# Loading parameter rows after the first transposes of x, and moving tile 7's first slabs, in a gated SSM + MLP kernel

## The chip, the cores and the metric

The kernel runs on one core of a Trainium2 chip. The metric is the device time of one execution in microseconds (us). A trace's span is 1.3 to 1.4 us shorter than the time of the same execution.

## The reference, cut to what matters

```
x: 2048 x 640, bf16                       # D = P = 640, F = 1728
g = sigmoid((x * gate_w).sum(-1))
dt = exp(log_dt); Lam_bar = exp(dt * (Lambda_re + i Lambda_im))
h[t] = Lam_bar * h[t-1] + (B_bar @ x[t])           # diagonal complex scan
a = 2 * Re(C @ h) + Dskip * x
b = gelu_tanh(x @ w1 + b1) @ w2 + b2
return g * a + (1 - g) * b
```

The parameters `Lambda_re`, `Lambda_im`, `log_dt` and `b1` are vectors. The kernel needs them as columns (one value per partition), so it loads them as rows and lets TensorE transpose them. A slab below is 128 of the 640 columns of x, or the 128 rows of w1 that go with them; a bank is one of the pieces of PSUM, the memory into which TensorE writes its results; a tile is one 128 x 512 result of the first product, kept in one bank.

## The kernel before: the parts that the change touches

Work is emitted by a list scheduler. Each `op(name, engine, modelled duration, reads, writes, emitter, prio)` becomes available when its inputs are, by modelled times; each engine takes the available op with the lowest `prio`. The order on each engine is therefore decided when the program is built, not on the chip.

The SyncE queue issues the large transfers in this order: x slabs 0 and 1 in natural layout, slabs 0 to 2 of W1 (256 KB each), then x slabs 2 to 4 by one DMA that transposes, then the rest of W1. ScalarE's queue issues the parameter rows at the very start.

```
load("xna", "sp", ...)                       # x[0:512], slabs 0 and 1, natural layout
w1load(0, "sp", 1); w1load(1, "sp", 1.3); w1load(2, "sp", 2)
xtrans(0, range(KN, KD), 3, 1.8)             # KN = 2: slabs 2..4 by a transposing DMA
w1load(3, "sp", 4); w1load(4, "sp", 5)
...
ROWS = {"lre": (0, A_Lambda_re), "lim": (KP, A_Lambda_im), "ldt": (2 * KP, A_log_dt), "b1a": (3 * KP, B_b1[0:nmain])}
op("rz", "pool", 0.2, (), list(ROWS) + ["b1b"], f_rz, prio=-90)            # zero the row tile
for i, (nm, (r0, src)) in enumerate(ROWS.items()):
    src = src.rearrange("(k p) -> k p", p=128)
    load(nm, "act", "l_" + nm, rows[r0:r0 + src.shape[0], :], src, [nm], prio=-100 + i, dur=0.4)
load("b1b", "pool", "l_b1b", rows[RT:RT + 1, :]..., ["b1b"], prio=-50, dur=1.0)   # tail of b1, as one more row
...
for i, (k, c0, c1) in enumerate(((0, 0, 2), (0, 2, 4), (1, 0, 4))):
    ...   # TensorE transposes x slabs 0 and 1 (8 blocks) into banks 7, 6, 5; VectorE copies them to xT
...
psC = PS[7][:, :].bitcast(BF16)[:, 0:128]
op("cols", "pe", 0.3, list(ROWS) + ["b1b", "ident"], [("bank", 7)], f_cols, prio=11.5)     # parameter transpose
op("cols1", "dve", 0.2, [("bank", 7)], ["lcol", "b1col"], f_cols1, prio=-1000)             # copy out of bank 7
op("dt", "act", ...)    # exp        then "ang" (VectorE), "amag" (exp), "psi" (VectorE), "sin" (two sines)
...
def m1_first():          # tiles 0..7 of x[0:512] @ W1, slab by slab, one PSUM bank per tile
    seq = [(k, jf) for k in range(KD) for jf in range(NW)]       # 5 slabs x 8 tiles = 40 matmuls
    seq.remove((0, NW - 1))
    seq.insert(seq.index((1, NW - 1)), (0, NW - 1))
    ...
    # then one GELU per tile on ScalarE; each frees its bank
```

The parameter transpose writes bank 7, which tile 7 also accumulates in, so tile 7 must wait until VectorE has copied the columns out. The ninth tile ("tile 8") reuses bank 0, so it must wait until the first GELU has read tile 0. And the exponentials and sines stand ahead of the first GELU on ScalarE, with two loads of the function table between them.

## Time and profile before

| | before |
|---|---|
| time, median of the runs (range) | 213.74 us (213.12 to 213.87) |
| TensorE busy | 209.3 of 212.3 us |
| parameter transpose starts | 7.61 us |
| first GELU starts | 12.62 us |
| tile 8 starts | 13.92 us |

The first line of the page's busy table (us, share of the span, instructions; PE is TensorE's matmuls, PEld its weight loads, DVE VectorE, ACT ScalarE, POOL GpSimd):

```profile
PE 209.3 (99%) x1264; PEld 120.6 (57%) x1264; DVE 189.2 (89%) x262; ACT 111.3 (52%) x201; POOL 3.0 (1%) x11
```

The waits of TensorE in the kernel before (engine, line, releaser: us in total, times, longest):

```profile
PE ps L399 <- PEq L960: 0.8, 1, 0.8
```

TensorE is the bound and waits for nothing once it has started. Its timeline over the first 15 us (start us, us, engine, line, operation, out<-in, shape, count):

```profile
3.75 1.03 PE L411 MATMUL ps<-ident,xn 128*128 128x128 bf16 x8
4.74 3.03 PE L619 MATMUL ps<-xT,W1sb 128*128 128x512 bf16 x11
7.61 0.22 PE L430 MATMUL ps<-ident,rows 128*128 128x128 bf16 x1
7.67 6.42 PE L619 MATMUL ps<-xT,W1sb 128*128 128x512 bf16 x29
13.92 1.24 PE L639 MATMUL ps<-xT,W1sb 128*128 128x512 bf16 x5
```

Eight transposes of x, 11 matmuls of the first pass, the parameter transpose, the other 29 matmuls, then tile 8 at 13.92.

The same stretch on ScalarE (a bracket gives the idle time before a line and its releaser; ACTq is ScalarE issuing a DMA):

```profile
0.97 0.55 ACTq L326 DMA_DIRECT2D rows<-in_A_Lambda_re_dram  x1
2.20 0.35 ACTq L326 DMA_DIRECT2D rows<-in_B_b_dram  x1
...
8.09 0.21 ACT L440 ACTIVATE dtb<-cols 128x5 bf16<-128x5 f32 x1 [4.23 <-DVE cols L435]
...
8.83 1.28 ACT L473 ACT_TABLE_LOAD   x1
...
10.78 1.28 ACT L628 ACT_TABLE_LOAD   x1
12.62 3.00 ACT L628 ACTIVATE Gl<-ps,cols 128x512 bf16<-128x512 f32 x5 [0.56 <-PE ps L619]
```

ScalarE was ready for the GELUs 0.56 us before TensorE had the first tile ready. The GELU ended at 13.30, 0.62 us before tile 8 needed its bank.

### The profile page before, as it was taken

What the parts mean: (1) busy time and instruction counts of PE and PEld (TensorE: products, weight loads), DVE (VectorE), ACT (ScalarE), POOL (GpSimd) and SP (SyncE); (2) the same over time, 40 slices, a digit from 0 to 9 for tenths busy, and PEclk for the clock granted to TensorE, in tenths of its full rate; (3) what the DMA queues carried; (4) which work ended last, traced back from release to release, by engine and by line L of the source; (5) the groups of instructions that cost most, each with busy time, mean ns of one, the idle gap of its engine ahead of it and who ended that gap; (6) DMA issues with size and microseconds to landing.
All of it is one profiled execution on the core that took longest, in us unless ns stands there. A gap on an engine that the chain in (4) does not pass through costs nothing.

```text
span 212.3 us, 3122 instructions
## 1 busy us (share of the span) xinstructions
PE 209.3 (99%) x1264; PEld 120.6 (57%) x1264; DVE 189.2 (89%) x262; ACT 111.3 (52%) x201; POOL 3.0 (1%) x11
## 2 busy tenths in 40 slices
PE   8999999999999999999999999999999999999995
PEld 3444444444567776444466777444446777767773
DVE  2499999999999999999999969899999999899443
ACT  2489556678905234556953233556792444722330
POOL 2000000000000010000000001000000000000000
DMA  5999799997000004100000014000000000010011
GB/s 147 316 263 203 161 221 317 274 213 173 24 0 3 31 31 127 62 0 0 0 3 0 0 36 154 31 31 3 0 0 2 3 31 31 31 34 0 31 34 62
DMA packets 31318, 16.35 MB, mean 77 GB/s; under 512 B 22984, under 2 KB 30408, under 8 KB 31304
## 3 DMA queue, kind: packets, MB, share of 16 engines
q1 hardware_dynamic: 30928, 14.83, 27.4%
q0 software_dynamic: 320, 1.31, 2.0%
q8 instruction: 10, 0.16, 0.3%
q14 instruction: 4, 0.03, 0.1%
q10 hardware_dynamic: 56, 0.01, 0.0%
HBM read 7.63 MB, written 2.62 MB: 48 GB/s over the span
## 4 chain that ended last, share of the span: by engine, by line
PE 99%; DVE 0%; issue 0%
PE ps L769 27%; PE ps L639 22%; PE ps L817 20%; PE ps L682 20%; PE ps L619 4%; PE ps L399 1%; PE ps L783 1%; PE ps L660 1%; PE ps L411 0%; DVE osb L850 0%; PE ps L430 0%
## 5 line engine op out<-in xcount | busy, mean ns | idle before, releaser
L769 PE MATMUL ps<-W2sb,Gl 128*128 128x320 bf16 x416 | 59.2, 299 | 0.0
L769 PEld LDWEIGHTS ps<-W2sb,Gl 128*128 128x128 bf16 x416 | 40.4, 98 | 17.0 <-issue 1.1
L639 PE MATMUL ps<-xT,W1sb 128*128 128x512 bf16 x220 | 48.1, 379 | 0.0
L817 PE MATMUL ps<-CT,H 128*128 128x320 bf16 (+2 forms) x320 | 45.4, 299 | 0.0
L722 DVE TENSOR_TENSOR_SCAN W<-atab,V 128x1280 bf16<-128x1280 f32 x16 | 44.3, 2811 | 0.3
L682 PE MATMUL ps<-xT,BT 128*128 128x512 bf16 x200 | 43.8, 379 | 0.0
L817 PEld LDWEIGHTS ps<-CT,H 128*128 128x128 bf16 x320 | 31.3, 98 | 12.2
L797 ACT ACTIVATE E<-ps,g1col 128x320 bf16<-128x320 f32 x32 | 16.3, 527 | 39.7 <-PE ps L769 25.5
L639 PEld LDWEIGHTS ps<-xT,W1sb 128*128 128x128 bf16 x220 | 21.6, 98 | 25.9
L646 ACT ACTIVATE Gl<-ps,cols 128x512 bf16<-128x512 f32 x44 | 29.6, 689 | 10.0 <-PE ps L639 10.0
L682 PEld LDWEIGHTS ps<-xT,BT 128*128 128x128 bf16 x200 | 19.4, 98 | 23.5 <-ACT Gt L668 0.4
L691 ACT ACTIVATE U<-ps 128x512 bf16<-128x512 f32 x40 | 23.8, 597 | 14.9 <-PE ps L682 14.9
L828 ACT ACTIVATE E<-ps,gcol 128x320 bf16<-128x320 f32 x30 | 15.8, 527 | 22.6 <-PE ps L817 22.6
L756 ACT ACTIVATE ps<-b2b 128x320 f32<-128x320 bf16 x32 | 14.1, 442 | 1.1
L480 DVE TENSOR_TENSOR osb<-xg,E 128x640 bf16<-128x640 bf16 x15 | 7.3, 488 | 7.9 <-ACT E L828 7.5
L836 DVE SCALAR_TENSOR_TENSOR xg<-xn,gcol,dsk 128x640 bf16<-128x640 bf16 x16 | 13.9, 883 | 0.4
L596 DVE SCALAR_TENSOR_TENSOR scr<-xn,gwb 128x640 bf16<-128x640 bf16 x16 | 13.2, 823 | 0.4
L480 DVE TENSOR_TENSOR V<-V,W 128x1280 bf16<-128x1280 bf16 x16 | 12.5, 821 | 0.3
L480 DVE TENSOR_TENSOR H<-H,V 128x1280 bf16<-128x1280 bf16 x16 | 12.5, 821 | 0.3
L480 DVE TENSOR_TENSOR V<-mr,U 128x2560 bf16<-128x2560 bf16 x8 | 11.9, 1489 | 0.2
L480 DVE TENSOR_TENSOR H<-c,W 128x2560 bf16<-128x2560 bf16 x8 | 11.9, 1490 | 0.2
L480 DVE TENSOR_TENSOR V<-s,W 128x2560 bf16<-128x2560 bf16 x8 | 11.9, 1484 | 0.0
(80 smaller groups left out, 100.2 us busy)
## 6 DMA issues: line engine op xcount, KB each, us to landing
out_dram<-osb SPq DMA_DIRECT2D x15, 160.0 KB, 1.8
W2sb<-in_B_w_dram SPq DMA_DIRECT2D x1, 2080.0 KB, 9.2
W1sb<-in_B_w_dram SPq DMA_DIRECT2D x5, 256.0 KB, 4.8
xn<-in_A_x_dram POOLq DMA_DIRECT2D x2, 640.0 KB, 4.7
xn<-in_A_x_dram SPq DMA_DIRECT2D x1, 640.0 KB, 7.7
W1sb<-in_B_w_dram SPq DMA_DIRECT2D x1, 480.0 KB, 5.8
W1sb<-in_B_w_dram SPq DMA_DIRECT2D x1, 400.0 KB, 6.4
xn<-in_A_x_dram SPq DMA_DIRECT2D x1, 384.0 KB, 6.0
```

Source lines behind the costliest of these rows:

```text
L480: return inc("dve", nc.vector.tensor_tensor(out=o, in0=a, in1=b, op=o_))
L639: t = nc.tensor.matmul(PS[bank][:, :], W1sb[:, k, jf * 128:(jf + 1) * 128], xT[q][:, k, :], start=(k == 0), stop=(k == KD - 1))
L646: return inc("act", nc.scalar.activation(Gl[q % 2][:, jf, :], PS[bank][:, :], ACT.Gelu_apprx_tanh, bias=b1col[:, jf:jf + 1]))
L682: t = nc.tensor.matmul(PS[bank][:, :], BT[:, ci, kd, k * 128:(k + 1) * 128], xT[q][:, kd, :], start=(kd == 0), stop=(kd == KD - 1))
L691: return inc("act", nc.scalar.activation(dst, src, ACT.Copy, scale=1.0 if ci == 0 else -1.0))
L722: t = inc("dve", nc.vector.tensor_tensor_scan(out=g[:, ci, :], data0=a, data1=v[:, ci, :], initial=0.0, op0=ALU.mult, op1=ALU.add))
L756: return inc("act", nc.scalar.activation(PS[bank][:, 0:HALF], b2b[:, cols], ACT.Copy))
L769: t = nc.tensor.matmul(PS[bank][:, 0:HALF], Gl[q % 2][:, jf, t4 * 128:(t4 + 1) * 128], W2sb[:, jf, cols], start=False, stop=False, skip_gr ...
L797: return inc("act", nc.scalar.activation(E1[c % NE][:, cols], PS[bank][:, 0:HALF], ACT.Copy, scale=g1col[:, c:c + 1]))
L817: t = nc.tensor.matmul(PS[bank][:, 0:n], H[b % NHB][:, ci, k, s * 128:(s + 1) * 128], CT[:, ci, k, cols], start=(i == 0), stop=(i == 2 * K ...
L828: return inc("act", nc.scalar.activation(E2[c % NE][:, cols], PS[bank][:, 0:HALF], ACT.Copy, scale=gcol[:, c:c + 1]))
L836: return inc("dve", nc.vector.scalar_tensor_tensor(out=xg[c % 2][:, :], in0=xn[q % 2][:, c % 4, :], scalar=gcol[:, c:c + 1], in1=dsk[:, :] ...
```

## The change

Its apparent intent: keep the small row loads out of the way of x at the start, give the first tiles to the slabs that arrive first, and write the tail of b1 straight into its column. The diff, cut to its core:

```
-        op("rz", "pool", 0.2, (), list(ROWS) + ["b1b"], f_rz, prio=-90)
-        for i, (nm, (r0, src)) in enumerate(ROWS.items()):
-            src = src.rearrange("(k p) -> k p", p=128)
-            load(nm, "act", ..., [nm], prio=-100 + i, dur=0.4)
-        load("b1b", "pool", "l_b1b", rows[RT:RT + 1, :]..., ["b1b"], prio=-50, dur=1.0)
+        op("rz", "pool", 0.2, (), list(ROWS), f_rz, prio=-90)
...
+            xts.append(op(f"xt{i}", "pe", ...))                  # the transposes of x
+        for i, (nm, (r0, src)) in enumerate(ROWS.items()):
+            load(nm, "act", ..., [nm], prio=-100 + i, dur=0.4, after=[xts[1]])
...
-        op("cols", "pe", 0.3, list(ROWS) + ["b1b", "ident"], [("bank", 7)], f_cols, prio=11.5)
+        op("cols", "pe", 0.3, list(ROWS) + ["ident"], [("bank", 7)], f_cols, prio=17.5)
...
-            return inc("dve", nc.vector.tensor_copy(out=cols[:, :], in_=psC[:, 0:RT + 1]))
+            return inc("dve", nc.vector.tensor_copy(out=cols[:, 0:RT], in_=psC[:, 0:RT]))
+        for i in range(2):                                       # cast loads into the column
+            load(f"b1b{i}", "pool", ..., cols[64 * i:64 * i + FL, RT:RT + 1], B_b1[nmain:F]..., [("b1t", i)],
+                 prio=-50 + i, dur=1.0, after=[cols1])
...
         def m1_first():
             seq = [(k, jf) for k in range(KD) for jf in range(NW)]
-            seq.remove((0, NW - 1))
-            seq.insert(seq.index((1, NW - 1)), (0, NW - 1))
+            for k in range(2):
+                seq.remove((k, NW - 1))
+                seq.insert(seq.index((2, 3)), (k, NW - 1))
```

TensorE's order, written as (slab, tile), goes from `(0,0..6) (1,0..3) cols (1,4..6) (0,7) (1,7) (2,0) ...` to `(0,0..6) (1,0..6) (2,0..2) cols (2,3) (0,7) (1,7) (2,4) ...`. The parameter transpose `cols` stands behind 17 matmuls in place of 11, and three of those 17 use slab 2.

More of the change, by code (lines that the diff above doesn't have):

```diff
@@ L321, in d_mm, with load @@
             return n / 2400.0 + 0.004
-        def load(name, eng, sem, dst, src, writes, prio, dur=0.5, lat=2.5, reads=(), **kw):
+        def load(name, eng, sem, dst, src, writes, prio, dur=0.5, lat=2.5, reads=(), after=()):
             def fn():
                 return dma_inc(eng, engines[eng].dma_start(dst, src), sem)
-            return op(name, eng, dur, reads, writes, fn, prio=prio, lat=lat)
+            return op(name, eng, dur, reads, writes, fn, prio=prio, lat=lat, after=after)
         def load_T(name, sem, pairs, writes, prio, dur, lat=3.0):
@@ L370, in f_rz @@
             return inc("pool", nc.gpsimd.memset(rows[:, :], 0.0))
-        op("rz", "pool", 0.2, (), list(ROWS) + ["b1b"], f_rz, prio=-90)
-        for i, (nm, (r0, src)) in enumerate(ROWS.items()):
-            src = src.rearrange("(k p) -> k p", p=128)
-            load(nm, "act", "l_" + nm, rows[r0:r0 + src.shape[0], :], src, [nm], prio=-100 + i, dur=0.4)
-        load("b1b", "pool", "l_b1b", rows[RT:RT + 1, :].rearrange("o (a p) -> o a p", a=2),
-             B_b1[nmain:F].rearrange("(o p) -> o p", o=1).unsqueeze(1).broadcast_to([1, 2, FL]), ["b1b"], prio=-50, dur=1.0)
+        op("rz", "pool", 0.2, (), list(ROWS), f_rz, prio=-90)
         def f_iota():
@@ L402, in bass_gated_mix__ssm_conv_s5__dense_activation_gelu__prompt_kernel @@
         op("warm", "pe", 2.7, (), [("bank", 4)], f_warm, prio=-1000)
-        for i, (k, c0, c1) in enumerate(((0, 0, 2), (0, 2, 4), (1, 0, 4))):
-            bank = 7 - i
+        xts = []
+        for i, (k, c0, c1, bank) in enumerate(((0, 0, 2, 7), (0, 2, 4, 6), (1, 0, 4, 5))):
             pt = PS[bank][:, :].bitcast(BF16)[:, 0:(c1 - c0) * 128]
@@ L412, in f_xt @@
                 return inc("pe", t)
-            op(f"xt{i}", "pe", 0.11 * (c1 - c0), ["xna", "ident"], [("bank", bank)], f_xt, prio=-990 + i)
+            xts.append(op(f"xt{i}", "pe", 0.11 * (c1 - c0), ["xna", "ident"], [("bank", bank)], f_xt, prio=-990 + i))
             def f_xc(k=k, pt=pt, c0=c0, c1=c1):
@@ L419, in bass_gated_mix__ssm_conv_s5__dense_activation_gelu__prompt_kernel @@
             op(f"xc{i}", "dve", 0.42, [("bank", bank)], [("xT", 0, k, c0)], f_xc, prio=-2000 + i)
+        for i, (nm, (r0, src)) in enumerate(ROWS.items()):
+            src = src.rearrange("(k p) -> k p", p=128)
+            load(nm, "act", "l_" + nm, rows[r0:r0 + src.shape[0], :], src, [nm], prio=-100 + i, dur=0.4, after=[xts[1]])
         XK0 = [[("xT", 0, k)] for k in range(KD)]
@@ L430, in f_cols @@
             return inc("pe", nc.tensor.transpose(psC, rows[:, :], ident[:, :]))
-        op("cols", "pe", 0.3, list(ROWS) + ["b1b", "ident"], [("bank", 7)], f_cols, prio=11.5)
+        op("cols", "pe", 0.3, list(ROWS) + ["ident"], [("bank", 7)], f_cols, prio=17.5)
         def f_cols1():
-            return inc("dve", nc.vector.tensor_copy(out=cols[:, :], in_=psC[:, 0:RT + 1]))
-        op("cols1", "dve", 0.2, [("bank", 7)], ["lcol", "b1col"], f_cols1, prio=-1000)
+            return inc("dve", nc.vector.tensor_copy(out=cols[:, 0:RT], in_=psC[:, 0:RT]))
+        cols1 = op("cols1", "dve", 0.2, [("bank", 7)], ["lcol", "b1col"], f_cols1, prio=-1000)
+        for i in range(2):
+            load(f"b1b{i}", "pool", f"l_b1b{i}", cols[64 * i:64 * i + FL, RT:RT + 1], B_b1[nmain:F].rearrange("(p o) -> p o", o=1), [("b1t", i)],
+                 prio=-50 + i, dur=1.0, after=[cols1])
         def f_dt():
@@ L669, in f_ge @@
                                                            bias=b1col[64 * i:64 * i + FL, NF - 1:NF]))
-                op(f"get_{q}_{i}", "act", d_act(512), [("bank", bank), "b1col"], [("gt", q + i, 0)], f_ge, prio=10)
+                op(f"get_{q}_{i}", "act", d_act(512), [("bank", bank), ("b1t", i)], [("gt", q + i, 0)], f_ge, prio=10)
                 load(f"gt{q + i}", "sp", f"l_gt{q + i}", Gt[q + i][64:64 + FL, :], Gt[q + i][0:FL, :], [("gt", q + i, 1)], 500, lat=2.5, reads=[("gt", q + i, 0)])
```

## The prediction

> **What bounds it now.** TensorE. The page's first part gives PE busy 209.3 of 212.3 us; the chain of waits is PE for 99%, nearly unbroken from 3.75 to 210.13 us. The waits view lists no PE wait but the 0.8 us before its first instruction. VectorE (89%) and ScalarE (52%) have room: in the timeline the first scan block's H is ready at 49.2 us, its projection starts at 65.1, and every later H is at least 7 us early. So only the first 14 us matter, and there only idle time of TensorE.
>
> **The start (timeline, single instructions).** The warm-up frees the array near 3.51 us (last matmul at 3.295, 256 columns at the slow pace of 0.427 per 512); x lands at 3.70, transposes start at 3.746: 0.23 us idle. The first real matmul starts at 4.738, 0.16 after the last transpose's slot. Matmuls come every 0.427 us until 5.57, every 0.216 from 5.88. The Trainium skill, "TensorE: Matmul & The Clock Gate" (the HAM clock gate), says a free-running activity window ends the half-speed phase; this step fits. A start earlier by g then buys about g/2.
>
> **What the change does.**
> 1. Four parameter loads leave the ScalarE queue at 0.97 to 2.55 us and are issued after the second transpose, about 4.4 to 5.8. They are small (packets of 18 ns); x may land 0.1 to 0.2 us sooner: gain 0.05 to 0.1. The DMA-transposed x (landed 8.58) may come 0 to 0.6 sooner: some w1 packets near 4 us took up to 1 us instead of 84 ns, but packets are also slow far from the row loads.
> 2. Rows took 2.2 to 3.5 us from issue to landing, so they land at 7.8 to 9.0.
> 3. The parameter transpose moves from after 11 first-pass matmuls to after 17; one matmul follows, then tile 7's two slabs, which use its bank. Before, VectorE's copy released the bank at 8.108, 0.5 us after the transpose (7.609), hidden by three matmuls. Now one hides 0.22: a new wait of 0.25 to 0.3.
> 4. Slab 2 is needed as the 15th matmul, not the 17th, at about 8.26. If the transposed x still lands at 8.58, PE waits 0.4 us; if 0.4 sooner, not.
> 5. The parameter chain starts 1.3 to 1.8 us later (transpose at 8.9 to 9.4). ScalarE's last table load ended 0.56 before the first GELU, which ended 0.6 before the matmul reusing its bank (13.92). The delay just uses that slack: 0 to 0.2 us. The scan chain moves too; the list scheduler answers with half a down-projection (1.8 us) before the first state projection, so no wait there.
> 6. The tail-bias cast loads come at about 9 us, needed near 46: free.
>
> **Sum.** -0.1, +0.28, +0 to 0.4, +0 to 0.2: about +0.2 to +0.4 us, allowing for the earlier landing. The runs of before spread over 0.75 us, more than the effect. Predicted 214.0 us, 8 in 10 within 213.0 to 214.9. Chances: faster by over 2% 0.01, within 2% 0.97, slower 0.02.
>
> **What would show it.** PE idle of about 0.25 us after the parameter transpose, released by VectorE's copy; that transpose at 8.9 to 9.4; idle before slab 2, released by the transposed x; unbroken PE after 15 us. Wrong if x lands as before (1), slab 2 comes without a wait (4), PE waits for the rows after the 17th matmul (2), or PE idles at the first state projection or later (5). The clock step can also move by itself.

## The result, and the profile after

| | before | after |
|---|---|---|
| time, median (range), 4 runs each | 213.74 us (213.12 to 213.87) | 215.0 us (214.66 to 215.2) |
| ratio of times | | 1.0063, 95% interval 1.0039 to 1.0087 |
| span of the profiled execution | 212.3 | 213.3 |
| last parameter row lands | 6.02 | 9.52 |
| parameter transpose starts | 7.61 | 9.65 |
| first GELU starts | 12.62 | 14.11 |
| tile 8 starts | 13.92 | 14.94 |

A ratio here is the mean time of one kernel's fast runs over that of the other's in the same rounds, so it is not quite the ratio of the medians. The changed kernel is 0.63% slower. That is within 2%, but its median lies just above the predicted range.

Busy time after (columns as before; ten matmul records are missing in this trace, so PE's sum is a little low):

```profile
PE 208.6 (98%) x1254; PEld 120.1 (56%) x1264; DVE 188.7 (88%) x262; ACT 111.2 (52%) x201; POOL 3.6 (2%) x12
```

The waits of TensorE in the changed kernel:

```profile
PE ps L393 <- PEq L962: 0.8, 1, 0.8
PE ps L621 <- DMA xT<-in_A_x_dram: 0.6, 1, 0.6
PE ps L621 <- DVE xT L411: 0.2, 1, 0.2
PE ps L684 <- issue: 0.2, 1, 0.2
```

The first line was there before. The last is most likely one of the missing records. The wait of 0.6 us for the DMA-transposed x is new. TensorE's timeline after:

```profile
4.61 3.46 PE L621 MATMUL ps<-xT,W1sb 128*128 128x512 bf16 x14 [0.19 <-DVE xT L411]
8.71 0.82 PE L621 MATMUL ps<-xT,W1sb 128*128 128x512 bf16 x3 [0.64 <-DMA xT<-in_A_x_dram]
9.65 0.22 PE L428 MATMUL ps<-ident,rows 128*128 128x128 bf16 x1
9.71 5.36 PE L621 MATMUL ps<-xT,W1sb 128*128 128x512 bf16 x22
```

The three matmuls of slab 2 start when the transposed x has landed (8.66), and the parameter transpose stands behind them. The waits view leaves out short waits. They show on the weight loads, which run just ahead of the matmuls (PEld of the changed kernel):

```profile
6.38 1.19 PEld L621 LDWEIGHTS ps<-xT,W1sb 128*128 128x128 bf16 x7 [0.58 <-DMA W1sb<-in_B_w_dram]
8.71 0.33 PEld L621 LDWEIGHTS ps<-xT,W1sb 128*128 128x128 bf16 x3 [1.14 <-DMA xT<-in_A_x_dram]
9.62 0.10 PEld L428 LDWEIGHTS ps<-ident,rows 128*128 128x128 bf16 x1 [0.59 <-issue]
...
10.14 4.43 PEld L621 LDWEIGHTS ps<-xT,W1sb 128*128 128x128 bf16 x22 [0.40 <-DVE cols L433]
```

A weight load is shorter than its matmul, so these idle times are longer than what TensorE really lost. Counting the matmul slots that stayed empty in the single instructions gives 0.25 us for W1 slab 1, 0.81 for slab 2 of x, 0.28 for the rows (landed 9.52) and 0.23 for bank 7. ScalarE after:

```profile
4.29 0.56 ACTq L326 DMA_DIRECT2D rows<-in_A_Lambda_re_dram  x1
5.52 0.32 ACTq L326 DMA_DIRECT2D rows<-in_B_b_dram  x1
...
10.12 0.21 ACT L441 ACTIVATE dtb<-cols 128x5 bf16<-128x5 f32 x1 [2.97 <-DVE cols L433]
...
10.87 1.28 ACT L474 ACT_TABLE_LOAD   x1
...
12.81 1.28 ACT L630 ACT_TABLE_LOAD   x1
14.11 1.84 ACT L630 ACTIVATE Gl<-ps,cols 128x512 bf16<-128x512 f32 x3
```

Here the first GELU carries no bracket: it starts right behind its table load. Before, it had waited 0.56 us for TensorE. The chain of waits of the changed kernel over the same stretch (start us, us, what) leads through the same waits; before, it was TensorE alone from 3.75 us on. After the transpose this view follows TensorE and not ScalarE, as the two paths end within 0.03 us of each other here (see the end of the experiments):

```profile
2.73 5.93 DMA xT<-in_A_x_dram
...
8.71 0.82 PE ps L621 x3
...
9.65 0.23 PE ps L428
...
9.90 0.20 DVE cols L433
...
10.15 3.41 PE ps L621 x15
...
13.61 1.46 PE ps L621 x6
15.07 5.43 PE ps L641 x25
```

From tile 8 on, both kernels run without a wait on TensorE. Tile 8 starts 1.02 us later (14.94 against 13.92) and the span is 1.0 us longer (213.3 against 212.3): the whole difference is made before 15 us. That bookkeeping held in every trace (table below). The traced execution of the changed kernel was the fastest of its four (214.66 us), so the trace shows less than the 1.26 us between the medians. So the question was what sets the start of tile 8.

### The profile page after: what moved, and what is told of

The parts are those of the page before. It is cut to its first block, busy times and chain, and to the rows that moved or that the text cites. A ratio compares the mean times of both kernels' runs of the same rounds, so it can differ in the third digit from the quotient of the medians.

```text
span 213.3 us, 3116 instructions
## 1 busy us (share of the span) xinstructions
PE 208.6 (98%) x1254; PEld 120.1 (56%) x1264; DVE 188.7 (88%) x262; ACT 111.2 (52%) x201; POOL 3.6 (2%) x12
## 4 chain that ended last, share of the span: by engine, by line
PE 94%; DMA 3%; SPq 1%; issue 1%; DVE 0%
PE ps L771 27%; PE ps L641 22%; PE ps L819 20%; PE ps L684 20%; DMA xT<-in_A_x_dram 3%; PE ps L621 3%; PE ps L785 1%; PE ps L662 1%; SPq L326 1%; DVE osb L852 0%; PE ps L428 0%; DVE cols L433 0%
## 5 line engine op out<-in xcount | busy, mean ns | idle before, releaser
L641 PE MATMUL ps<-xT,W1sb 128*128 128x512 bf16 x215 | 47.5, 379 | 0.3
L684 PE MATMUL ps<-xT,BT 128*128 128x512 bf16 x196 | 43.1, 379 | 0.3 <-issue 0.2
L481 DVE TENSOR_TENSOR W<-mi,U 128x2560 bf16<-128x2560 bf16 x8 | 11.9, 1484 | 0.0
```

Of the source, the lines that this page charges most:

```text
L481: return inc("dve", nc.vector.tensor_tensor(out=o, in0=a, in1=b, op=o_))
L641: t = nc.tensor.matmul(PS[bank][:, :], W1sb[:, k, jf * 128:(jf + 1) * 128], xT[q][:, k, :], start=(k == 0), stop=(k == KD - 1))
L684: t = nc.tensor.matmul(PS[bank][:, :], BT[:, ci, kd, k * 128:(k + 1) * 128], xT[q][:, kd, :], start=(kd == 0), stop=(kd == KD - 1))
```

## The experiments

Each call of experiments ran all its kernels and the kernel before on one chip, in the same rounds. There were five rounds for every kernel, and each has five or six runs, one of them profiled. The median of the kernel before was between 213.47 and 213.81 us. Runs of different calls are compared below only through their ratios to before. For o and p, eleven of the twelve runs of before are those of the call ahead of theirs, on the same chip. All results were correct.

Theory T, held at first, says that the loss is the sum of TensorE's new waits: for slab 2, for the rows, for bank 7. The rival that came to replace it says that the parameter chain (transpose, copy, exponential, sines, table loads, first GELU, bank 0) became the longest path, whatever TensorE waits for on the way. For the late landing of the rows there were two rules: Q, the transfers are served strictly in the order of issue, and L, a load takes a fixed latency.

| kernel | median us | ratio to before (95%) | parameter transpose | tile 8 | span |
|---|---|---|---|---|---|
| before | 213.74 | | 7.61 | 13.92 | 212.3 |
| changed | 215.0 | 1.0063 (1.0039 to 1.0087) | 9.65 | 14.94 | 213.3 |
| a_cast_only | 213.53 | 0.9997 (0.9985 to 1.001) | 7.28 | 13.84 | 212.2 |
| c_rows_late_only | 215.63 | 1.0088 (1.007 to 1.0105) | 11.46 | 16.75 | 215.1 |
| d_after_rows_early | 214.41 | 1.0031 (1.0019 to 1.0043) | 9.45 | 14.74 | 213.1 |
| h_after_seven_later | 215.68 | 1.0113 (1.0082 to 1.0145) | 11.19 | 17.89 | 216.2 |
| i_after_again | 215.57 | 1.0098 (1.0081 to 1.0116) | 10.50 | 15.79 | 214.1 |
| e_after_xt_split | 214.59 | 1.0047 (1.0032 to 1.0062) | 9.99 | 15.28 | 213.6 |
| f_after_rows_early_xt_split | 213.43 | 0.9998 (0.9984 to 1.0013) | 8.41 | 13.70 | 212.0 |
| j_rows_mid | 214.21 | 1.0035 (1.002 to 1.005) | 9.06 | 14.36 | 212.7 |
| g_before_xt_split | 213.32 | 0.9995 (0.9979 to 1.001) | 8.05 | 14.36 | 212.7 |
| k_before_xt_first | 213.8 | 1.0011 (0.9995 to 1.0027) | 8.12 | 14.44 | 212.8 |
| m_before_x_two_loads | 213.91 | 1.0014 (1.0 to 1.0028) | 7.60 | 13.91 | 212.3 |
| n_early_split_seven_later | 213.76 | 1.001 (0.9995 to 1.0026) | 8.93 | 14.22 | 212.6 |
| o_before_chain_longer | 214.13 | 1.0032 (1.0015 to 1.0048) | 7.46 | 14.63 | 213.0 |
| p_before_chain_bit_longer | 213.78 | 1.0012 (0.9998 to 1.0025) | 7.9 | 14.46 | 212.8 |

The last three columns are of the one profiled execution. The span moves with tile 8 one for one: c, for example, is 2.83 us later at tile 8 and 2.8 longer. The profiled execution need not be a typical one: the step of TensorE's clock from half to full speed fell between 3.8 and 6.8 us, and tile 8 of the kernels with the old order and the old chain moved between 13.84 and 14.44, mostly with it.

### a: the kernel before, with the cast loads only

```
-load("b1b", "pool", ..., rows[RT:RT + 1, :]..., ["b1b"], ...)
+for i in range(2): load(f"b1b{i}", "pool", ..., cols[64*i:64*i+FL, RT:RT+1], ..., after=[cols1])
```

> The kernel before with the two cast loads of the tail bias alone. Theory T (TensorE's own first-pass order: slab 2 too early for the transposed x, then the rows, then the bank): no part of it is in here, so 0 us against before, within 0.2, TensorE unbroken from 5.9 us on. Rival C (the element-wise cast loads slow the weight stream or VectorE): 0.3 us slower or more.

The ratio was 0.9997. The loads land at 13.8 to 14.0 us and are needed near 46 us. They cost nothing that these runs can show.

### c: the kernel before, with late row loads only

```
-load(nm, "act", ..., prio=-100 + i, dur=0.4)
+load(nm, "act", ..., prio=-100 + i, dur=0.4, after=[xts[1]])
```

> The kernel before with the late parameter rows alone: seventh tile and priority of the parameter transpose as before, tail bias still by the row. The scheduler's order on TensorE comes out the same as in the changed kernel (17 matmuls, transpose, one matmul, tile 7's two). Theory T: the whole loss, 1.0 to 1.3 us slower than before, with waits for the transposed x (0.4 to 0.8), the rows (about 0.3) and the bank (about 0.2). A rival that the edit of the seventh tile's order costs something by itself expects half of that or less.

The ratio was 1.0088. The scheduler gave TensorE the same order as in the changed kernel, since late rows make `cols` available late; the edits of the tile order decide nothing here. The last row landed at 11.22 us, 5.3 us after its issue. TensorE's waits:

```profile
PE ps L432 <- DMA rows<-in_B_b_dram: 1.6, 1, 1.6
...
PE ps L621 <- DMA xT<-in_A_x_dram: 0.3, 1, 0.3
```

That is about 1.9 us slower, more than the 1.0 to 1.3 expected, as the wait for the rows was 1.77 us and not 0.3. Late rows by themselves, with the order that the scheduler then chooses, bring the whole loss.

### d: the changed kernel, with the rows loaded early again

```
-load(nm, "act", ..., after=[xts[1]])
+load(nm, "act", ...)
```

> The changed kernel with the rows loaded at the start again, order on TensorE unchanged. Theory T: only the wait for the rows goes (0.28 us in the trace of after); the wait for the transposed x (until 8.6 to 8.7) and for the bank (0.22) stay: 0.7 to 0.9 us slower than before. Rival D (the late row packets, at 7.5 to 9.0 us, delay the transposed x and the weights): all of it goes, within 0.2 of before, and the transposed x lands clearly earlier.

The ratio fell to 1.0031, about half the changed kernel's 1.0063. The rows are there, but the transpose still starts at 9.45 us, because it stands behind three matmuls of slab 2:

```profile
PE ps L621 <- DMA xT<-in_A_x_dram: 0.5, 1, 0.5
```

Transposed x landed at 8.74 us, no sooner than in the changed kernel (8.66), so rival D falls. Two things then make the transpose late: its place behind slab 2, and rows that land later still.

### h: the changed kernel, tile 7 two matmuls later

```
-seq.insert(seq.index((2, 3)), (k, NW - 1))
+seq.insert(seq.index((2, 6)), (k, NW - 1))
```

> The changed kernel with tile 7's first two slabs two matmuls further behind (three matmuls between the parameter transpose and tile 7 instead of one). Theory T: the wait for the bank (0.22 us) goes, the waits for the transposed x and the rows stay: 0.8 to 1.05 us slower than before, about 0.2 faster than the changed kernel. If the bank wait were only the shadow of something else, the same as the changed kernel (1.0 to 1.3).

This was meant to hide the bank wait. Three matmuls now stand between the parameter transpose and tile 7, in place of one. Its trace shows no bank wait, but the ratio was 1.0113, where 0.8 to 1.05 us had been expected. Two of the six runs (217.63 and 217.26 us) had a mean granted clock of 0.992 in place of 1.0. Without these two the mean is 1.0085 times that of before, which lies between the changed kernel's two ratios (1.0063, and 1.0098 in i), so h does not decide what the bank wait costs. The windows view of the first of them (window: length; busy us and instructions of PE, PEld, DVE, ACT, POOL; granted clock; DMA share; GB/s):

```profile
4.44:7.85 3.41, 3.11 (x18) 1.26 (x16) 0.76 (x3) 0.18 (x1) 0.00 (x0) 1.00 1.06 199
7.85:11.26 3.41, 1.45 (x8) 0.38 (x7) 0.00 (x0) 1.10 (x1) 0.00 (x0) 1.00 1.10 353
11.26:14.68 3.42, 3.42 (x10) 1.18 (x10) 2.78 (x9) 2.59 (x6) 1.25 (x2) 0.50 1.24 308
14.68:18.10 3.42, 3.42 (x17) 1.54 (x16) 3.17 (x23) 2.48 (x4) 0.00 (x0) 1.00 1.12 185
```

In the second window TensorE was busy for only 1.45 of 3.41 us, as it waited for slab 2 (0.71 us lost) and for the rows (1.58). The clock then fell to one half for the next 3.41 us, although TensorE was busy all through it. The Trainium skill ("TensorE: Matmul & The Clock Gate", the HAM clock gate) gives a free-running window of 4096 cycles for this gate; the half-speed stretch in this trace is 3413 ns. Matmuls spaced 0.427 us instead of 0.216 over it cost about 1.7 us. The kernel c waited 1.77 us for its rows without such a fall. That its wait lay across a window's border does not explain this: from the spacing of c's matmuls its clock stepped up at about 6.2 us (an estimate), so windows of the same length counted from there hold the whole wait in one, 9.65 to 13.07, with TensorE busy for 1.74 of 3.42 us. That is little more than h's 1.45. Why the clock fell in h and not in c stays open; one execution of each was traced.

### i: the changed kernel again

> The changed kernel once more, for a second trace beside the others of this call. 0.9 to 1.6 us slower than before. Theory Q (small loads get no way past the SP engine's large ones: they land with what SP issued just before them): the last row load lands at about 9.5 us if it is issued before the load of W1's columns 1024 to 1407, and at about 11 if after it; the wait for the rows is about 0.3 us or about 1.6 accordingly.

Run in another call, the same kernel had the ratio 1.0098: twice the distance of before. The trace says why (waits of TensorE, then the chain):

```profile
PE ps L428 <- DMA rows<-in_B_b_dram: 0.8, 1, 0.8
...
PE ps L621 <- DMA xT<-in_A_x_dram: 0.2, 1, 0.2
```

```profile
5.76 4.61 DMA rows<-in_B_b_dram
...
10.50 0.23 PE ps L428
```

The rows landed at 10.37 us instead of 9.52. That is 0.85 us later, and it matches the 0.85 us by which tile 8 moved (15.79 against 14.94). All five runs of i (215.38 to 216.16 us) lie above all four of the first session (214.66 to 215.2), so the difference lies between the two more than between executions. Rule Q had named 9.5 us or about 11 for the last row, according to its place ahead of or behind SyncE's load of W1's columns 1024 to 1407; it was issued behind it (5.76 against 5.69 us) and landed between the two values.

### e: the changed kernel, transposing load split

```
-xtrans(0, range(KN, KD), 3, 1.8)
+xtrans(0, range(KN, KN + 1), 3, 0.7)      # slab 2 by itself
+xtrans(0, range(KN + 1, KD), 3.1, 1.2)
```

> The changed kernel with the DMA transpose of x split in two, slab 2 first. Slab 2 lands earlier than 8.6 us. Theory T (waits in a row, the later one takes over what the earlier one frees): the wait before slab 2 shrinks, the wait for the rows grows by as much, so the time stays that of the changed kernel within 0.3 us (0.9 to 1.8 us slower than before). Rival S (the transposed x alone sets the time): faster than the changed kernel by what slab 2 gains, 0.4 us or more.

Slab 2 now landed at 7.51 us and its wait vanished. The wait for the rows took its place:

```profile
PE ps L429 <- DMA rows<-in_B_b_dram: 1.4, 1, 1.4
```

The ratio was 1.0047. As theory T expected, the wait moved to the rows and a loss of 1.0 us remains. But i, the changed kernel in the same call, had 1.0098, so e is about 1.0 us faster than the changed kernel, as rival S expected and T did not. The rows landed sooner too: at 9.86 us against 10.37 in i, 3.4 to 3.9 us after their issue against 4.5 to 4.6, and tile 8 is 0.51 us sooner. So e took away about half of the loss, and its one trace, of the slowest of its six runs, does not tell slab 2's share from the rows'.

### f: both causes undone

d and e together: early rows and the split load.

> The changed kernel with the rows at the start again and the DMA transpose of x split, slab 2 first. Theory T: no wait for rows, the wait before slab 2 (0.67 us in the run with early rows) shrinks by what slab 2 lands earlier, the bank wait (0.23) stays: within 0.4 us of before, at least 0.3 faster than with early rows alone (0.66 slower than before).

The ratio was 0.9998. The transpose starts at 8.41 us. The new order, the bank wait (0.23 us) and the cast loads are all still there, and the loss is gone.

### j: the rows issued in between

```
+constop = op("const", "dve", ...)          # the identity is made
-load(nm, "act", ..., after=[xts[1]])
+load(nm, "act", ..., after=[constop])
```

> The changed kernel with the rows issued once the identity is made, at about 2.0 to 3.4 us, around SP's loads of W1 slabs 1 and 2 and the transposed x. Theory Q (landing in order of issue across the two queues): the first row load lands at 6.3 to 7.2 us, the last, issued after the transposed x, at 8.5 to 9.3. Rival L (a small load lands a fixed 2.2 to 3.6 us after its issue): first at 4.2 to 5.6, last at 5.5 to 7. Either way no wait or a short one for the rows at TensorE (needed at 9.4), so the time is that of the changed kernel with early rows: 0.5 to 0.9 us slower than before.

The rows were issued at 2.01 to 3.24 us and landed at 4.87 to 7.50, so the latency was 2.9 us for the first and 4.3 to 4.4 for the other three. Rule Q expected the last at 8.5 to 9.3, rule L at 5.5 to 7; it came at 7.50. Neither holds as stated. The rows no longer bind; the transpose stands behind three matmuls of slab 2, for which TensorE waits 0.15 us, and the ratio is 1.0035, about that of d.

### g, k and m: attempts at a version that beats both

g is the kernel before with the split of e. In k, slab 2's transposing load is also issued ahead of W1 slab 2. In m, the split is kept and x slabs 0 and 1 come as two loads, the second after W1 slab 0.

```
g:  +xtrans(0, range(KN, KN + 1), 3, 0.7); +xtrans(0, range(KN + 1, KD), 3.1, 1.2)
k:  +xtrans(0, range(KN, KN + 1), 1.6, 0.7); the rest as g
m:  g, and load("xna0") ahead of w1load(0), load("xna1") behind it
```

> The kernel before with its DMA transpose of x split in two, slab 2 first. The kernel before needs slab 2 at about 8.6 to 8.7 us, just when it lands, so theory T expects at most the short wait seen there (0 to 0.23 us) to go: 0 to 0.25 us faster than before, none in a run whose clock steps up late.

> As the split on the kernel before, but slab 2 is issued ahead of W1's slab 2 on the SP queue. Slab 2 of x lands earlier still, W1's slab 2 later; both are needed for the same matmul, so the same as the plain split, 0 to 0.25 us faster than before.

> As the split on the kernel before, and the first x slab loads in two pieces, so that the first two groups of transposes need half the bytes. The first piece may land 0.2 to 0.4 us sooner than 3.8; what is gained there is halved where TensorE is still at half speed: 0.1 to 0.4 us faster than before, unless the extra issue of 0.45 us on SP delays W1's slabs 1 and 2 enough to wait for.

The ratios were 0.9995, 1.0011 and 1.0014; every interval touches or includes 1. In g's and k's traces TensorE has no wait after its first matmul of W1; their tile 8 is late mainly because the clock step fell late (6.75 and 6.83 us). In m the first piece of x landed at 3.03 us, some 0.7 us sooner, but the second came at 4.91; its transposes stood behind three matmuls, and TensorE then lost 0.25 us until VectorE had copied them out of the bank that tile 5 needs. The gain expected of m did not come. No version beats the kernel before.

### n: f, and tile 7 two matmuls later

The edit of h on top of f: no slab wait, no row wait, and now no bank wait either.

> The changed kernel with early rows, split transpose of x, and tile 7 two matmuls further behind: the bank wait by itself, which the run with late rows could not show. Theory T: the bank wait (0.23 us in the run with early rows and split) goes and nothing takes its place: 0.1 to 0.3 us faster than before. If the bank wait only hides another: 0 (the same as early rows and split).

Here T failed: taking away the bank wait gained nothing (1.001 against before, where T expected 0.1 to 0.3 us faster; f had 0.9998). TensorE in n's timeline:

```profile
8.93 0.22 PE L429 MATMUL ps<-ident,rows 128*128 128x128 bf16 x1
8.98 5.13 PE L622 MATMUL ps<-xT,W1sb 128*128 128x512 bf16 x22
14.22 1.46 PE L642 MATMUL ps<-xT,W1sb 128*128 128x512 bf16 x6
```

All the matmuls behind the transpose run without a gap, and then tile 8 loses 0.27 us waiting for the first GELU, whose signal came at 14.08. From the transpose to tile 8 it takes 5.29 us, exactly as in the changed kernel (9.65 to 14.94) and in c, d, e, f, i and j (5.28 to 5.30). The new order alone, with its clock step (5.79 us) near that of before (5.88), thus starts the transpose 1.32 us later, six matmul slots, and tile 8 0.30 us later; the interval of n's ratio holds both this and zero. In f's trace the step came at 3.96 us, so that tile 8 was early all the same.

### o and p: the kernel before with a longer parameter chain

What was still open was whether the chain alone, with nothing else changed, costs this time and has the slack it seems to have. One idle activation, whose result is not used, stands ahead of the sines: 2145 columns in o, 660 in p.

```
 def f_sin():
+    inc("act", nc.scalar.activation(dly, psi.broadcast(...), ACT.Sin, scale=0.5))
     inc("act", nc.scalar.activation(sh[:, :, :], psi[:, :, :], ACT.Sin, scale=0.5))
```

> The kernel before with nothing moved, but one idle activation of 2145 columns (about 2 us) put into ScalarE's parameter chain before its sines. Theory P (the eighth... that is, the first matmul of tile 8, starts no sooner than 5.29 us after the parameter transpose, because the first GELU must free its bank; in before that leaves 1.02 us of slack): with the chain about 2 us longer, tile 8 starts at about 14.9 instead of 13.9 us, released by ScalarE's GELU, and the kernel is 0.7 to 1.1 us slower: most of the change's loss with no late row, no new order and no bank wait. Rival W (the loss is the sum of the waits seen before slab 2, the transpose and tile 7): none of these is in here, so 0, within 0.25.

> The same with an idle activation of 660 columns (about 0.7 us). Theory P: the slack of 1.02 us takes it all, so 0, within 0.25 us. If ScalarE's chain cost in proportion (no slack): about 0.4 us or more.

The waits of TensorE in o, and ScalarE's timeline:

```profile
PE ps L641 <- ACT Gl L630: 0.5, 1, 0.5
```

```profile
10.03 2.00 ACT L474 ACTIVATE H<-tr 128x2145 bf16<-128x2145 f32 x1
...
12.50 1.28 ACT L630 ACT_TABLE_LOAD   x1
13.80 1.84 ACT L630 ACTIVATE Gl<-ps,cols 128x512 bf16<-128x512 f32 x3
```

The added activation took 2.00 us (the Trainium skill, "ScalarE: Activation LUTs", What ACT_TABLE_LOAD costs, gives 186 ns + 0.833 ns per column for an activation with immediate scale and bias, from which one estimates 1.97) and lengthened the chain by 1.90, as the next activation overlaps its end. With the transpose at 7.46 and 5.29 us of chain, tile 8 should start at 7.46 + 5.29 + 1.90 = 14.65; it started at 14.63, behind a wait for the GELU, and the ratio was 1.0032, or 0.68 us, where the record had 0.7 to 1.1 and tile 8 at about 14.9. No late row, no new order and no bank wait is in this kernel. In p the chain is 0.66 us longer: tile 8 does not wait for the GELU, and the ratio is 1.0012 with 1 inside the interval. In p's one trace TensorE itself was later at tile 8 (14.46 us), and not for its clock, which stepped up at 5.06: W1's slab 1 landed at 7.01 us (6.40 in before) and the transposed x at 9.22 (8.58). So the ratio over the rounds is the better witness here. TensorE's wait for W1 in p:

```profile
PE ps L621 <- DMA W1sb<-in_B_w_dram: 0.5, 1, 0.5
```

This fits a slack between 0.66 us and 1.90, as the trace's 1.0 says.

### What the experiments add up to

Tile 8 starts 5.29 us after the parameter transpose whenever the transpose is late. In the kernel before, the transpose at 7.61 would allow tile 8 at 12.90; TensorE itself gets there only at 13.92, which leaves 1.02 us of slack. For a late transpose the loss is its delay less 1.02:

| kernel | delay of the transpose | less 1.02 | tile 8 later by |
|---|---|---|---|
| changed | 9.65 - 7.61 = 2.04 | 1.02 | 1.02 |
| d (rows early) | 1.84 | 0.82 | 0.82 |
| i (changed, again) | 2.89 | 1.87 | 1.87 |
| c (rows late only) | 3.85 | 2.83 | 2.83 |

The last two columns agree because the 5.29 us are the same in every one of these traces; they are no second check of it.

One point stays undecided in the changed kernel itself. TensorE's own path from the late transpose to tile 8 (the bank wait and 22 matmuls) takes 5.26 us, within 0.03 of the chain. In that kernel either would nearly do. The chain ends last, though: in the changed kernel and in c, d, e, f, i, j, n and o tile 8 starts 0.14 to 0.15 us after the end of the first GELU, and in the others, where TensorE's own work sets it, 0.62 us after. But only n, where the matmul path was shortened, and o, where the chain alone was lengthened, show that the chain binds by itself.

What makes the rows land late is settled only in part. In the traces of late rows with the whole transposing load their packets moved only as the transposing load's packets ended: in the changed kernel the first row packet of the late loads moved at 7.56 us, 3.3 us after its issue, and the transposing load's packets ended at 8.00; in i the two times are 8.05 and 8.31, in c 8.23 and 8.48. In the kernel before, the first load was issued at 0.97 and its first packet moved at 2.40. In j, whose rows were issued around the transposing load, 42 of their 56 packets moved between its first packet (5.42 us) and its last (7.85). j agrees with the Trainium skill, "DMA: Bandwidth & Descriptors" (Issuing engines are not separate DMA queues): transfers issued by different engines run on the same 16 DMA engines and interleave. In those traces of late rows, a small load did not get round the backlog by being on another engine's queue. Part of the variation may be the place against SyncE's load of W1's columns 1024 to 1407: the last row landed at 9.52 us where it was issued ahead of that load (the changed kernel, 5.52 against 5.84), and at 10.37, 11.05 and 11.22 where it was issued behind it (i, 5.76 against 5.69; h, 5.79 against 5.61; c, 5.89 against 5.50). No run changed this place alone, so it is not shown. Why j's rows came sooner than strict order of issue would have it, and what else makes the landing vary, stays open.

## Why the prediction was right or wrong

**Bound and place: right.** TensorE bounds both kernels, and the whole difference lies in the first 15 us. After 15 us the changed kernel has no new wait.

**Step 1, x lands 0.1 to 0.2 us sooner, transposed x 0 to 0.6 sooner: wrong.** Natural x landed at 3.65 to 3.85 us in the nine traces with early rows that load it in one piece, and at 3.58 to 3.83 in those with late or middle rows. The transposed x landed at 8.58 before and 8.66 after. The intended gain is not there. A sooner start would have bought nothing anyway, as slab 2's landing pins the order: in the changed kernel's trace the clock step came early (4.03 us), and the time so won was lost again in waits for W1 (0.25) and slab 2 (0.81).

**Step 2, rows land at 7.8 to 9.0: wrong.** They landed at 9.52 in the first trace, 10.37 in the second, 11.2 in c. The latency of the start (1.9 us for the first row load, 3.8 for the fourth; the prediction read 2.2 to 3.5) was carried over to a moment when a transposing load and several 256 KB loads had been issued ahead; there it was 4.0 to 5.3 us (3.4 to 3.9 behind the split load of e). It brought a wait for the rows, 0.28 us and 0.98 us in the two traces, that the sum did not hold. The prediction did name it as a way to be wrong.

**Step 3, bank wait of 0.25 to 0.3: right in size, 0.23 us.** But it is not a cost of its own: n took it away and gained nothing.

**Step 4, wait of 0.4 us for slab 2: right in kind.** It was 0.40 in i and 0.81 in the first trace, where the early clock step brought TensorE to slab 2 sooner.

**Step 5, the parameter chain "just uses that slack: 0 to 0.2 us": this is the step that failed.** The mechanism was seen, and both parts of the slack were read rightly from the trace (0.56 and 0.6 us, less 0.14: 1.02). But its own delay of 1.3 to 1.8 us less that slack makes 0.3 to 0.8, not 0 to 0.2, and with the true delay of 2.04 to 2.89 the term is 1.02 to 1.87. This one term is the whole difference at tile 8. The transpose was expected at 8.9 to 9.4 and came at 9.65 and 10.50.

**The sum.** The prediction added waits along TensorE to the delay of the chain. They are not separate: the waits for slab 2 and for the rows come ahead of the transpose and are what delays it. The right form is one path, start of the transpose + 5.29 us against 13.92. With the predicted transpose at 8.9 to 9.4 it would have given +0.3 to +0.8 us, and with the measured one +1.0. Measured were +1.26 us of the medians in the first session, and +2.1 in the second. That the sum came as near as it did is luck: the bank wait of 0.28 us, which n shows to be no cost, and the wait for slab 2 stood in for part of the chain's term.

**Step 6, cast loads free: right.** Shown by a.

## What to carry to other kernels

Before moving a small load or transpose later "because its result is needed late", follow its result to the next thing the bound engine needs, here a PSUM bank freed by the first GELU, and compare the delay with the slack of that whole chain as one path. Don't take a small load's latency from the idle start: here, behind large and transposing transfers, it landed 4.0 to 5.3 us after issue instead of 1.9 to 3.8. And a wait on the bound engine is not a loss by itself: taking one away pays only if no equal path stands behind it (n).

## What the Trainium skill lacked or had wrong

- "DMA: Bandwidth & Descriptors", Issuing engines are not separate DMA queues, says that transfers of different engines interleave, and the section Latency and other measured facts speaks of a fixed cost near 2 us. It gives no figure for what a load of 1 to 3 KB meets behind a backlog: it landed 1.9 us after issue as the first one at the start, but 4.0 to 5.3 us after issue behind a transposing load and 256 KB loads, and this varied by 0.85 us between two traces of one kernel.
- "TensorE: Matmul & The Clock Gate", HAM oscillation and Why this matters for your kernels, speak of idle gaps of more than about 3 or 3.4 us as what throttles the clock; the section A second HAM failure mode adds frequent micro-idles, without a figure. The page lacks how little busy time in a window is enough. In h the clock fell to one half for 3413 ns after a window in which TensorE was busy 1.45 of 3.41 us and no single gap was longer than 1.58 us; by the mean clock of 0.992 it did so in two of six runs. In c, 1.74 us busy of 3.42 in a window placed by an estimate were not followed by a fall.
- "ScalarE: Activation LUTs", What ACT_TABLE_LOAD costs, gives 1283 ns for the load and some 1380 ns more for a drain. The traces agree on the load (1.28 us), but show no such drain: the load starts 0.01 to 0.02 us after the activation ahead of it ended, and the next activation starts 0.01 to 0.08 us after it (in the changed kernel an activation ends at 12.80, the load runs from 12.81 to 14.09, the GELU starts at 14.11). A switch of tables cost 1.3 us here.
